# The last pair of token blocks of a fused recurrence and maxout layer as seven products, with stores by column halves

## The chip, the cores and the metric

The kernel runs on one core of one Trainium2 chip. The time is the device time of one execution in microseconds (us); medians of a few executions are quoted. Ratios are the mean time of one kernel's runs over that of the other's of the same rounds on the same chip, so they are not quite the ratio of the quoted medians. The span of a profile is about 1.8 us shorter than the timed value of the same execution. "Landing" means the moment at which a store's semaphore has had its last update, as the trace records it.

Engines in the profile: PE is TensorE (PEld its weight loads), DVE is VectorE, ACT is ScalarE, POOL is GpSimd, SP is SyncE, which here only issues DMAs and closes the program.

## The reference, cut to what matters

```python
# x, f_logit: (4, 6144, 256), lower_bound: (256,)
f = lower_bound + (1 - lower_bound) * sigmoid(f_logit)
h = 0
for t in range(S):                      # a gated recurrence over time
    h = f[:, t] * h + (1 - f[:, t]) * x[:, t]
    y[:, t] = h
# then, per token, with w1, w2: (256, 1024), w_out: (1024, 256)
g = maximum(y @ w1, y @ w2)
out = g @ w_out                         # (24576, 256) float32
```

The kernel writes the maximum as `y @ w1 + relu(y @ (w2 - w1))`. So the second layer has ten slices of 128 in its contraction: eight of ReLU outputs and two of `y` itself, whose weights `w13` are `w1 @ w_out`.

## The kernel before: the parts that matter here

Tokens go in blocks of 512. The second layer of two blocks, `ja` and `jb`, is one 2x2 by 2x2 block product: rows are the two blocks, the contraction is cut into two halves of five slices each, and the output columns into `lo` (0 to 127) and `hi` (128 to 255). That takes seven products of 20 matmuls of 128x128 in place of eight (the Strassen-Winograd scheme). A product adds into one bank of PSUM, the memory that matmuls write their sums to; the banks are named here X, B and E. VectorE makes four sums of left operands per pair, and `t1` to `t4` are sums of weights made once.

```python
def sevenths(p):
    ...
    product("X", part(0, 0), plain(0, lo), True)      # M1
    then(seed("B", "X"))                              # ACT: B = X
    product("E", sub(1), given(t1), True)             # M5
    then(snapshot("E", 5))                            # ACT: copy to SBUF
    product("X", sub(2), given(t2))                   # M6
    then(snapshot("X", 2))
    product("B", part(0, 1), plain(1, lo))            # M2: ja, lo is ready
    then(leave("B", ja, lo, None, False))
    product("X", sub(3), given(t3))                   # M7: jb, hi = X + snapshot 5
    then(leave("X", jb, hi, 5, False))
    product("E", sub(4), plain(1, hi))                # M3: ja, hi = E + snapshot 2
    then(leave("E", ja, hi, 2, True))
    product("X", part(1, 1), given(t4))               # M4: jb, lo
    then(leave("X", jb, lo, None, True))
```

The products of pair p are interleaved with the first layer of pair p + 1. The last pair has no successor and was done plainly instead, 40 matmuls of 128x256 per block; the last block was stored in four pieces of 128 KB, each as soon as its group of 128 tokens was copied:

```python
for step in queue: step()              # the rest of the pair before the last
for j in (NBLK - 2, NBLK - 1):
    for slot in range(FC):
        second_layer(j, slot)
# in second_layer, last block only, after the ten matmuls of token group i:
(nc.vector.tensor_copy if r else nc.scalar.copy)(out=osb[:, i:i+1, :], in_=ps[:, r:r+1, :])
store(j, osb, i, 1, nc.sync if r else nc.scalar)
```

## Time and profile before

The median was 380.87 us (three runs, 380.62 to 381.02). The page of the profile has the busy shares and the shares of the chain of waits that ended last:

```profile
span 379.8 us, 9454 instructions
...
PE 369.1 (97%) x4076; PEld 279.9 (74%) x4076; DVE 333.0 (88%) x402; ACT 300.3 (79%) x406; POOL 37.5 (10%) x79
...
PE 89%; DMA 4%; DVE 3%; POOL 1%; SPq 1%; ACT 0%; issue 0%
```

TensorE is busy 97% of the span and is 89% of the chain, so matmul work taken away should show, if it lies on the chain's end too. The chain from 360 us on (start, us, what):

```profile
365.36 1.51 PE ps L605 x27
366.87 8.75 PE ps L482 x80
375.62 0.02 issue
375.64 0.42 DVE osb L491
```

L605 is the matmul of the seven products, L482 the plain second layer. 27 narrow matmuls took 1.51 us, 56 ns each; the 80 wide ones took 8.75 us, 109 ns each. After the last VectorE copy (376.06) nothing is left but the last store and the closing, until 379.8. The timeline has the last ReLU and the last two copies (start, us, engine, line, what, and in brackets the idle time before it and who ended it):

```profile
365.40 1.02 ACT L444 ACTIVATE r<-dT 128x1024 f16<-128x1024 f32 x1 [0.79 <-PE dT L436]
...
374.55 0.37 ACT L491 COPY osb<-ps 128x256 f32<-128x256 f32 x1 [1.81 <-PE ps L482]
...
375.64 0.42 DVE L491 COPY osb<-ps 128x256 f32<-128x256 f32 x1 [1.76 <-PE ps L482]
```

These groups of the page give the durations of what the change adds: a sum, a snapshot and an add (after the shapes, the count, the busy us and the ns of one):

```profile
L506 DVE TENSOR_TENSOR S<-r 128x2560 f16<-128x2560 f16 x42 | 62.4, 1485 | 10.1 <-ACT r L444 10.0
...
L562 DVE TENSOR_TENSOR osb<-ps,sn 128x512 f32<-128x512 f32 x42 | 28.7, 684 | 6.8 <-ACT osb L560 5.3
...
L550 ACT COPY sn<-ps 128x512 f32<-128x512 f32 x42 | 24.6, 587 | 1.1 <-PE ps L605 0.9
```

Last, the end of the kernel in windows of half a microsecond; of each line the last three numbers matter, the granted clock, the mean busy share of the 16 DMA engines, and GB/s:

```profile
375.40:375.90 0.50, 0.20 (x2) 0.00 (x0) 0.26 (x1) 0.00 (x0) 0.00 (x0) 1.00 0.15 55
375.90:376.40 0.50, 0.00 (x0) 0.00 (x0) 0.16 (x1) 0.00 (x0) 0.00 (x0) 1.00 0.59 207
376.40:376.90 0.50, 0.00 (x0) 0.00 (x0) 0.00 (x0) 0.00 (x0) 0.00 (x0) 1.00 0.00 0
376.90:377.40 0.50, 0.00 (x0) 0.00 (x0) 0.00 (x0) 0.00 (x0) 0.00 (x0) 1.00 0.74 262
```

The DMA engines stand still from 376.4 to 376.9. The last store, issued at 376.09, then has them for itself.

### The profile page before, as it was taken

The numbers are of one execution on the slowest core, as the hardware profiler recorded it, in microseconds if no ns is written. First come the engines' busy times: TensorE is split into PE (matmuls) and PEld (weight loads), VectorE is DVE, ScalarE is ACT, GpSimd is POOL, SyncE is SP. The second block draws the span as 40 slices with busy tenths as digits, with TensorE's granted clock in tenths as the row PEclk, the third lists the DMA queues.
The fourth block names the chain that finished last, engine by engine and source line by source line (L and its number), as shares of the span: only waits on it lengthen the run. The fifth ranks groups of instructions, "written<-read, shape, count | busy, mean of one in ns | idle before, by whom it ended". The sixth has DMA issues, their size and how long they took to land.

```text
span 379.8 us, 9454 instructions
## 1 busy us (share of the span) xinstructions
PE 369.1 (97%) x4076; PEld 279.9 (74%) x4076; DVE 333.0 (88%) x402; ACT 300.3 (79%) x406; POOL 37.5 (10%) x79
## 2 busy tenths in 40 slices
PE   4999999999999999999999999999999999999995
PEld 3677766777777777777777777777777777777784
DVE  4696789999999999999999999999999999999721
ACT  4846788798798888888888887987888888888740
POOL 1500103101201101102011011011011021000000
PEclk9999999999999999999999999999999999999999
DMA  7994999989999999999899999999999999970223
GB/s 249 242 226 98 265 162 256 167 156 289 195 195 276 180 190 251 202 172 285 143 257 190 219 251 278 127 263 223 182 263 212 188 268 211 192 265 3 110 113 113
DMA packets 103389, 77.17 MB, mean 203 GB/s; under 512 B 93554, under 2 KB 94066, under 8 KB 102642
## 3 DMA queue, kind: packets, MB, share of 16 engines
q1 hardware_dynamic: 100514, 51.13, 59.8%
q0 software_dynamic: 2544, 25.17, 34.5%
q8 instruction: 32, 0.52, 0.6%
q10 hardware_dynamic: 288, 0.26, 0.2%
q14 instruction: 11, 0.09, 0.1%
HBM read 53.48 MB, written 48.23 MB: 268 GB/s over the span
## 4 chain that ended last, share of the span: by engine, by line
PE 89%; DMA 4%; DVE 3%; POOL 1%; SPq 1%; ACT 0%; issue 0%
PE ps L605 42%; PE dT L436 41%; PE ps L482 6%; DMA xT<-in_x_dram 3%; DMA r<-in_moe_w_dram 1%; DVE r L230 1%; DVE S L506 1%; SPq L117 0%; PE ps L180 0%; DVE osb L496 0%; DVE v L223 0%; POOL fT L105 0%; DVE ff L213 0%; ACT r L444 0%; POOL wob L631 0%
## 5 line engine op out<-in xcount | busy, mean ns | idle before, releaser
L444 ACT ACTIVATE r<-dT 128x1024 f16<-128x1024 f32 x192 | 195.8, 1022 | 53.2 <-PE dT L436 53.0
L436 PE MATMUL dT<-r,wd 128*128 128x512 f16 x768 | 225.4, 379 | 1.0 <-DVE wd L360 0.5
L605 PEld LDWEIGHTS <-S 128*128 128x128 f16 x1680 | 110.9, 101 | 37.6 <-issue 0.6
L605 PEld LDWEIGHTS <-r 128*128 128x128 f16 x1260 | 87.3, 101 | 36.6
L230 DVE TENSOR_TENSOR_SCAN r<-ff,r,v 128x512 f16<-128x512 f16 x88 | 108.2, 1270 | 0.8
L605 PE MATMUL ps<-t,S 128*128 128x128 f16 x1260 | 97.8, 219 | 0.0
L436 PEld LDWEIGHTS <-wd 128*128 128x128 f16 x768 | 67.6, 113 | 6.4 <-DVE wd L360 1.1
L506 DVE TENSOR_TENSOR S<-r 128x2560 f16<-128x2560 f16 x42 | 62.4, 1485 | 10.1 <-ACT r L444 10.0
L605 PE MATMUL ps<-wob,r 128*128 128x128 f16 x672 | 67.4, 219 | 0.0
L506 DVE TENSOR_TENSOR S<-r,S 128x2560 f16<-128x2560 f16 x42 | 61.9, 1474 | 0.0
L285 ACT ACTIVATE u<-fT 128x512 f16<-128x512 f16 x88 | 56.0, 636 | 1.0 <-DMA fT<-scr 1.0
L213 DVE TENSOR_SCALAR ff<-u,nom 128x512 f16<-128x512 f16 (+1 forms) x98 | 31.3, 346 | 9.7 <-ACT u L207 5.3
L348 POOL CAST waited<-fT 128x1 f32<-128x1 f16 x21 | 10.8, 513 | 279.5 <-DMA fT<-scr 279.5
L605 PE MATMUL ps<-w,r 128*128 128x128 f16 x168 | 36.8, 219 | 0.0
L562 DVE TENSOR_TENSOR osb<-ps,sn 128x512 f32<-128x512 f32 x42 | 28.7, 684 | 6.8 <-ACT osb L560 5.3
L605 PE MATMUL ps<-t,r 128*128 128x128 f16 x420 | 33.4, 219 | 0.0
L605 PE MATMUL ps<-wob,S 128*128 128x128 f16 x336 | 31.4, 219 | 0.0
L223 DVE TENSOR_TENSOR v<-u,xT 128x1024 f16<-128x1024 f16 x44 | 30.1, 684 | 0.2 <-DMA xT<-scr 0.2
L482 PEld LDWEIGHTS <-r 128*128 128x128 f16 x240 | 23.9, 101 | 6.9
L482 PE MATMUL ps<-wob,r 128*128 128x256 f16 x192 | 26.8, 273 | 0.0
L550 ACT COPY sn<-ps 128x512 f32<-128x512 f32 x42 | 24.6, 587 | 1.1 <-PE ps L605 0.9
L560 ACT COPY osb<-ps 128x512 f32<-128x512 f32 x42 | 24.4, 582 | 0.5 <-PE ps L605 0.5
(56 smaller groups left out, 134.8 us busy)
## 6 DMA issues: line engine op xcount, KB each, us to landing
out_dram<-osb SPq DMA_DIRECT2D x47, 512.0 KB, 3.9
scr<-in_f_logit_dram POOLq DMA_DIRECT2D x22, 512.0 KB, 7.4
scr<-in_x_dram POOLq DMA_DIRECT2D x22, 512.0 KB, 10.4
r<-in_moe_w_dram SPq DMA_DIRECT2D x4, 512.0 KB, 6.8
fT<-in_f_logit_dram POOLq DMA_DIRECT2D x3, 256.0 KB, 9.2
xT<-in_x_dram POOLq DMA_DIRECT2D x3, 256.0 KB, 11.1
osb<-in_f_logit_dram SPq DMA_DIRECT2D x2, 256.0 KB, 4.5
osb<-in_x_dram SPq DMA_DIRECT2D x2, 256.0 KB, 4.1
```

The lines of the kernel that those rows point to most:

```text
L213: nc.vector.tensor_scalar(out=ff[:, h, cols], in0=u[:, h, cols], scalar1=nom[:, h : h + 1], scalar2=1.0, op0=ALU.mult, op1=ALU.add,)
L223: nc.vector.tensor_tensor(out=like(v[:, :, cols], xT), in0=like(u[:, :, cols], xT), in1=xT, op=ALU.mult,)
L230: nc.vector.tensor_tensor_scan(out=y_of(j, h), data0=ff[:, h, o : o + TB], data1=v[:, h, o : o + TB], initial=0.0 if t0 == 0 else y_of(j - ...
L285: nc.scalar.activation(out=mids[p + NBLK, "u"][:, h, cols], in_=held[c, 0][:, h, cols], func=AF.Sigmoid, scale=-1.0,)
L436: nc.tensor.matmul(dT[:, fc % 2, :], lhsT=wd[:, kc, unit_cols(fc)], rhs=y_of(j, kc), start=(kc == 0), stop=(kc == KC - 1),)
L444: nc.scalar.activation(out=rts[j, k][:, g - 1 : g + 1, :].rearrange("p q (i m) -> p q i m", m=P), in_=dT[:].rearrange("p q (m i) -> p q i ...
L482: nc.tensor.matmul(ps[:, r, :], lhsT=left, rhs=right, start=(s == 0 and (r == 0 or j == NBLK - 1)), stop=(s == n - 1 and (r == 1 or j == N ...
L506: nc.vector.tensor_tensor(out=t[:], in0=a, in1=b, op=op)
L550: nc.scalar.copy(out=t[:], in_=bank[b][:])
L560: nc.scalar.copy(out=dst, in_=bank[b][:])
L562: nc.vector.tensor_tensor(out=dst, in0=bank[b][:], in1=snap[name][:], op=ALU.add)
L605: nc.tensor.matmul(bank[b][:, i, :], lhsT=a[:, k, cols], rhs=w, start=fresh, stop=after is not None, skip_group_check=True,)
```

## The change

The last pair becomes seven products as well. Its order is M1 M5 M2 M6 M3 M7 M4, so that each sum is ready in time. M4 does not add into bank X but goes to banks of its own; X is copied to a snapshot after M7, and `jb, lo` is formed in three adds as M4's token groups finish. Outputs leave by column halves, in pieces of 512 B. The third sum of the last pair is made while the first layer still runs.

```diff
-    def store(j, osb, first=0, n=TB // P, queue=None):
+    def store(j, osb, groups=slice(0, TB // P), cols=slice(0, D), queue=None):
 ...
+        end = p == NPAIR - 1
 ...
-                if last:
+                if end:
+                    store(j, osbs[j], cols=cols)
+                elif last:
                     store(j, osbs[j])
+        def leave_both(b):
+            def go():
+                leave(b, jb, hi, 5, False)()
+                snapshot(b, 4)()
+        def leave_last(i):
+            at = slice(0, 2) if i == 1 else slice(i, i + 1)
+            def go():
+                nc.vector.tensor_tensor(out=osbs[jb][:, at, lo],
+                    in0=bank["Y"][:, at, 0:P], in1=snap[4][:, at, :], op=ALU.add)
+                store(jb, osbs[jb], at, lo, nc.scalar if i == 2 else nc.sync)
 ...
+        if end:
+            product("B", part(0, 1), plain(1, lo))     # M2
+            then(leave("B", ja, lo, None, False))
+            product("X", sub(2), given(t2))            # M6
+            then(snapshot("X", 2))
+            product("E", sub(4), plain(1, hi))         # M3
+            then(leave("E", ja, hi, 2, True))
+            product("X", sub(3), given(t3))            # M7
+            then(leave_both("X"))
+            product("Y", part(1, 1), given(t4))        # M4, groups 0 and 1, 2, 3 in three banks
+            ... leave_last(1), (2), (3) after groups 1, 2, 3
 ...
-        for j in (NBLK - 2, NBLK - 1):
-            for slot in range(FC):
-                second_layer(j, slot)
+        sum1(p); sum2(p); sum4(p)
+        for step in sevenths(p):
+            step()
```

More of the change, by code (lines that the diff above doesn't have):

```diff
@@ L456, in store @@
             out=out[r0 : r0 + nb, :].rearrange("(p n) d -> p n d", p=P)[
-                :, first : first + n, :
+                :, groups, cols
             ],
-            in_=osb[:, first : first + n, :],
+            in_=osb[:, groups, cols],
         )
@@ L470, in second_layer @@
             g, r = divmod(i, 2)
-            if s == 0 and (r == 0 or j == NBLK - 1):
+            if s == 0 and r == 0:
                 acc["ps"] = ps_o.tile([P, 2, D], FP32, name="ps")
@@ L485, in second_layer @@
                 rhs=right,
-                start=(s == 0 and (r == 0 or j == NBLK - 1)),
-                stop=(s == n - 1 and (r == 1 or j == NBLK - 1)),
+                start=(s == 0 and r == 0),
+                stop=(s == n - 1 and r == 1),
                 skip_group_check=True,
             )
-            if j == NBLK - 1 and s == n - 1:
-                (nc.vector.tensor_copy if r else nc.scalar.copy)(
-                    out=osb[:, i : i + 1, :], in_=ps[:, r : r + 1, :]
-                )
-                store(j, osb, i, 1, nc.sync if r else nc.scalar)
-            elif r == 1 and s == n - 1:
+            if r == 1 and s == n - 1:
                 (nc.scalar.copy if j == 0 else nc.vector.tensor_copy)(
@@ L536, in then, with open_bank @@
             steps[-1][-1] = fn
-        def open_bank(b):
-            bank[b] = ps_o.tile([P, TB // P, P], FP32, name="ps")
+        def open_bank(b, i=0):
+            if i:
+                t = ps_d.tile([P, 2 * TB // P, P], FP32, name="dT")
+            else:
+                t = ps_o.tile([P, TB // P, P], FP32, name="ps")
+            bank[b] = t
         def seed(b, src):
@@ L564, in go @@
                     )
-                if last:
+                if end:
+                    store(j, osbs[j], cols=cols)
+                elif last:
                     store(j, osbs[j])
+            return go
+        def leave_both(b):
+            def go():
+                leave(b, jb, hi, 5, False)()
+                snapshot(b, 4)()
+            return go
+        def leave_last(i):
+            at = slice(0, 2) if i == 1 else slice(i, i + 1)
+            def go():
+                nc.vector.tensor_tensor(
+                    out=osbs[jb][:, at, lo],
+                    in0=bank["Y"][:, at, 0:P],
+                    in1=snap[4][:, at, :],
+                    op=ALU.add,
+                )
+                store(jb, osbs[jb], at, lo, nc.scalar if i == 2 else nc.sync)
             return go
@@ L585, in sevenths @@
         then(snapshot("E", 5))
-        product("X", sub(2), given(t2))
-        then(snapshot("X", 2))
-        product("B", part(0, 1), plain(1, lo))
-        then(leave("B", ja, lo, None, False))
-        product("X", sub(3), given(t3))
-        then(leave("X", jb, hi, 5, False))
-        product("E", sub(4), plain(1, hi))
-        then(leave("E", ja, hi, 2, True))
-        product("X", part(1, 1), given(t4))
-        then(leave("X", jb, lo, None, True))
+        if end:
[8 more added lines that the diff above has]
+            product("Y", part(1, 1), given(t4))
+            for i in range(TB // P):
+                steps[(i - TB // P) * (KH + 1)][-2] = i != 1
+                if i:
+                    steps[(i - TB // P + 1) * (KH + 1) - 1][-1] = leave_last(i)
+        else:
+            product("X", sub(2), given(t2))
+            then(snapshot("X", 2))
+            product("B", part(0, 1), plain(1, lo))
+            then(leave("B", ja, lo, None, False))
+            product("X", sub(3), given(t3))
+            then(leave("X", jb, hi, 5, False))
+            product("E", sub(4), plain(1, hi))
+            then(leave("E", ja, hi, 2, True))
+            product("X", part(1, 1), given(t4))
+            then(leave("X", jb, lo, None, True))
         def runner(step):
@@ L601, in run @@
                 if fresh:
-                    open_bank(b)
+                    open_bank(b, i)
                 a = left()
@@ L715 @@
             more = p + 1 < NPAIR
-            seq = [(27, scans[p]["scan10"]), (36, scans[p]["scan11"])]
+            seq = [
+                (27, scans[p]["scan10"]),
+                (36, scans[p]["scan11"]),
+                (112, lambda: sum3(p)),
+            ]
             if more:
@@ L723 @@
                     (84, scans[p + 1]["scan01"]),
-                    (112, lambda: sum3(p)),
                     (131, scans[p + 1]["decay1"]),
@@ L753 @@
             step()
-        for j in (NBLK - 2, NBLK - 1):
-            for slot in range(FC):
-                second_layer(j, slot)
+        p = NPAIR - 1
+        sum1(p)
+        sum2(p)
+        sum4(p)
+        for step in sevenths(p):
+            step()
 _INS = ['x', 'f_logit', 'lower_bound', 'moe_w1', 'moe_w2', 'moe_w_out']
```

## The prediction

> **What bounds the kernel now.** TensorE. On the page it is busy 97% of the span, and the chain of waits that ended last is 89% TensorE; in the windows from 300 us on it is busy without a gap. Only the end changes. The chain of 360-381 us reads: seven-product matmuls until 366.87, then 80 second-layer matmuls of 128x256 (8.75 us, 109 ns each) for the last two blocks, then a 424 ns VectorE copy until 376.06, then nothing but the last store and the closing: store issued 376.09, its 1 KB packets 376.93-377.44, landed 377.99, span end 379.77. So 3.7 us of tail follow the last copy.
>
> **What the change removes.** The 80 wide matmuls. Added are 140 of 128x128; in the same trace a run of 27 of these takes 1.51 us, 56 ns each, so 140 take 7.8 us. Matmul work saved: 0.95 us.
>
> **What it adds.**
> 1. Four sums on VectorE (1.48 us each). The third is moved into the last pair, where VectorE idles 5.3 us (timeline 358.6-363.9): free. The first needs the last ReLU, which ends 366.42. It runs about 366.45-367.94, while the first product (20 matmuls, 1.1 us from 366.65) is done at about 367.77: TensorE waits about 0.2 us before M5. The second (to 369.35) and fourth (to 370.75) are ready before M6 (370.3) and M7 (371.4). M2 before M6 is there for that.
> 2. A serial end. M3 ends about 373.75. VectorE adds out of its bank (0.69 us), and only then may ScalarE copy the same bank to the snapshot (0.59 us): the built program shows the copy waiting for VectorE. That is the rule of the Trainium skill, "PSUM — Partial Sum Buffer", section "PSUM bank collisions raise a hardware error": two engines may not read one bank at once. No run here shows a collision. So the snapshot is there at about 375.1. M4, in banks of its own, ends at 374.85 without waiting, and the adds of its groups queue behind the snapshot: 128x256 (estimate 0.42), then two of 128x128 (estimate 0.28 each, overlapping by 0.09 as VectorE neighbours do here): last one done about 375.95. TensorE ends 0.75 us earlier, but the last VectorE instruction only 0.1 us earlier.
> 3. Stores by column halves with 512 B pieces: 1 KB packets take 45 ns, 4 KB 160, so about 26 ns for 512 B (estimate); 256 KB is 0.8 us over 16 engines, not limiting. The last store is 64 KB in place of 128 KB, about 0.25 us less between first packet and landing, and its semaphore is checked one place later in the closing's list (0.07 us).
>
> **Sum.** 0.95 saved by matmuls, minus 0.2 (M5 wait), minus 0.6 (snapshot chain), plus 0.3 (smaller last store, closing): about 0.45 us, or 0.1%. All before 362 us is the same instruction stream.
>
> **Prediction: 380.4 us**, 8 in 10 between 379.9 and 380.9. Chances: faster by over 2% 0.005, within 2% 0.99, slower by over 2% 0.005.
>
> **What would show each step right.** No 128x256 matmuls after 367 us; 140 at a 56 ns pace; one TensorE gap of about 0.2 us before M5, released by the first sum, no other over 0.1 us; in the timeline VectorE add, ScalarE snapshot, VectorE adds back to back at the end, the chain of waits running through them; last VectorE end 0.1 us before that of the old kernel; last landing about 0.3 us earlier.
>
> **What would make it wrong.** The sum arriving later (a slower ReLU or leave ahead of it); 512 B pieces that cost more, or stores queued behind each other (each issue took 0.33 us), so that the last one lands later; semaphore hops above the 0.03 us seen between ReLU and sum[...].

(Two names are swapped in it: what it calls M7 and M3 are M3 and M7 in the names of the change. The instructions and times it means are the fifth and the sixth product.)

## The result

The changed kernel took 381.01 us (median of 4 runs, 380.54 to 381.83), before 380.87 (4 runs, 380.62 to 381.02): ratio 1.0007, 95% interval 0.9988 to 1.0025. That is 0.11 us outside the range predicted, with runs of one kernel that lie 1.3 us apart. A second set of six runs had a median of 380.66 us, inside that range, but before then had 380.69, ratio 1.0002 (0.9986 to 1.0017). So the part to explain is not the 0.1 us of the median: it is that the gain of 0.45 us is not there. The timed runs alone cannot exclude it (a gain of 0.45 us would be a ratio of 0.9988, the edge of both intervals); the traces have to show it.

The profiled spans, 379.8 us before and 379.1 after, seem to say that it is. They mislead. Matching ScalarE's activations of both traces one by one, the changed kernel is 0.66 us ahead at 27 us, long before any instruction that was changed, and still exactly 0.66 us ahead at the last ReLU: 365.40 and 364.74 us. Over the twelve other traces that lead over the trace of before lies between 0.21 and 0.97 us and is there by 27 us each time. The opening, which waits for the first loads, makes it: 0.47 us of it is the same in all twelve and arises between 22 and 26 us, where in the trace of before alone TensorE waits for a load of x. That execution took 381.55 us, more than any of the four timed runs of before. From here on every time is therefore counted from the start of the last ReLU of its own trace. From there to the end of the span it is 14.37 us before and 14.33 after.

The chain of the changed kernel at its end:

```profile
367.34 5.77 PE ps L642 x100
373.12 0.02 issue
373.14 0.70 DVE osb L562
373.84 0.02 issue
373.87 0.60 ACT sn L550
374.46 0.02 issue
374.48 0.42 DVE osb L582
```

And its timeline, with the last ReLU, the one gap of TensorE, and the end:

```profile
364.74 1.02 ACT L444 ACTIVATE r<-dT 128x1024 f16<-128x1024 f32 x1 [0.79 <-PE dT L436]
...
367.34 1.14 PEld L642 LDWEIGHTS <-S 128*128 128x128 f16 x20 [0.17 <-DVE S L501]
...
373.14 0.69 DVE L562 TENSOR_TENSOR osb<-ps,sn 128x512 f32<-128x512 f32 x1 [0.37 <-PE ps L642]
373.50 0.72 PE L642 MATMUL dT<-t,r 128*128 128x128 f16 x10
373.87 0.59 ACT L550 COPY sn<-ps 128x512 f32<-128x512 f32 x1 [2.37 <-DVE osb L562]
374.48 0.42 DVE L582 TENSOR_TENSOR osb<-ps,sn 128x256 f32<-128x256 f32 x1 [0.65 <-ACT sn L550]
374.83 0.48 DVE L582 TENSOR_TENSOR osb<-dT,sn 128x128 f32<-128x128 f32 x2
375.14 0.37 ACTq L455 DMA_DIRECT2D out_dram<-osb  x1
```

This much is as predicted: one TensorE gap of 0.17 us before M5 released by the first sum, then no gap; M4 done at 374.22; VectorE add, ScalarE snapshot and VectorE adds back to back. The windows of the DMA engines are not:

```profile
374.74:375.24 0.50, 0.00 (x0) 0.00 (x0) 0.50 (x3) 0.00 (x0) 0.00 (x0) 1.00 0.71 203
375.24:375.74 0.50, 0.00 (x0) 0.00 (x0) 0.07 (x1) 0.00 (x0) 0.00 (x0) 1.00 0.95 282
375.74:376.24 0.50, 0.00 (x0) 0.00 (x0) 0.00 (x0) 0.00 (x0) 0.00 (x0) 1.00 0.97 293
376.24:376.74 0.50, 0.00 (x0) 0.00 (x0) 0.00 (x0) 0.00 (x0) 0.00 (x0) 1.00 0.89 281
376.74:377.24 0.50, 0.00 (x0) 0.00 (x0) 0.00 (x0) 0.00 (x0) 0.00 (x0) 1.00 0.33 98
```

Where before they stood still ahead of the last store, they are now at work without a break from about 375.1 to 377.0, at 281 to 293 GB/s.

The account, in us after the start of the last ReLU. The two measured columns come from the traces' records; the predicted one is worked out from the prediction's times minus 365.40 (its landing: 12.60, less 0.10 for the adds and 0.25 for the store):

| | before | predicted | after |
|---|---|---|---|
| TensorE done | 10.21 | 9.45 | 9.48 |
| last copy or add done | 10.67 | 10.55 | 10.57 |
| last store issued | 10.69 | | 10.69 |
| last packet done | 12.03 | | 12.28 |
| last landing | 12.60 | 12.25 | 12.67 |
| end of the span | 14.37 | 13.9 | 14.33 |

TensorE is done 0.73 us earlier, of which 0.10 us reaches the last add: right. From the last add to the landing it takes 2.10 us, where 1.93 less 0.25, or 1.68, was predicted: 0.42 us more. The closing, 1.78 us before, is 1.66 us. So the 0.04 us that the stage gains are 0.10 (adds) less 0.17 (stores) plus 0.12 (closing).

### The profile page after: what moved, and what is told of

The parts are those of the page before. It is cut to its first block, busy times and chain, and to the rows that moved or that the text cites. A ratio compares the mean times of both kernels' runs of the same rounds, so it can differ in the third digit from the quotient of the medians.

```text
span 379.1 us, 9589 instructions
## 1 busy us (share of the span) xinstructions
PE 367.8 (97%) x4136; PEld 279.5 (74%) x4136; DVE 338.9 (89%) x407; ACT 302.6 (80%) x409; POOL 34.9 (9%) x79
## 4 chain that ended last, share of the span: by engine, by line
PE 91%; DVE 5%; DMA 1%; ACT 1%; SPq 0%; issue 0%; DVEq 0%
PE ps L642 44%; PE dT L436 41%; PE ps L482 4%; DVE r L230 1%; DMA osb<-in_f_logit_dram 1%; DVE S L501 1%; PE ps L180 1%; DVE wd L360 1%; DVE v L223 0%; PE ps L392 0%; DVE ff L213 0%; DVE osb L491 0%; ACT r L444 0%; DVE r L264 0%; SPq L117 0%
## 5 line engine op out<-in xcount | busy, mean ns | idle before, releaser
L642 PEld LDWEIGHTS <-S 128*128 128x128 f16 x1760 | 115.4, 101 | 37.9 <-issue 0.6
L642 PEld LDWEIGHTS <-r 128*128 128x128 f16 x1320 | 90.8, 101 | 36.6
L642 PE MATMUL ps<-t,S 128*128 128x128 f16 x1320 | 101.6, 219 | 0.0
L501 DVE TENSOR_TENSOR S<-r 128x2560 f16<-128x2560 f16 x44 | 65.4, 1486 | 14.5 <-ACT r L444 14.4
L642 PE MATMUL ps<-wob,r 128*128 128x128 f16 x704 | 69.8, 219 | 0.0
L501 DVE TENSOR_TENSOR S<-r,S 128x2560 f16<-128x2560 f16 x44 | 65.1, 1479 | 0.0
L642 PE MATMUL ps<-w,r 128*128 128x128 f16 x176 | 38.5, 219 | 0.0
L348 POOL CAST waited<-fT 128x1 f32<-128x1 f16 x21 | 8.7, 413 | 280.0 <-DMA fT<-scr 280.0
L550 ACT COPY sn<-ps 128x512 f32<-128x512 f32 x45 | 26.4, 587 | 4.6 <-DVE osb L562 2.4
L482 PEld LDWEIGHTS <-r 128*128 128x128 f16 x160 | 16.0, 101 | 6.2
L642 PE MATMUL ps<-w,S 128*128 128x128 f16 x88 | 19.3, 219 | 0.0
## 6 DMA issues: line engine op xcount, KB each, us to landing
xT<-in_x_dram POOLq DMA_DIRECT2D x3, 256.0 KB, 10.3
```

The costliest lines, as they stand in the source:

```text
L482: nc.tensor.matmul(ps[:, r, :], lhsT=left, rhs=right, start=(s == 0 and r == 0), stop=(s == n - 1 and r == 1), skip_group_check=True,)
L501: nc.vector.tensor_tensor(out=t[:], in0=a, in1=b, op=op)
L550: nc.scalar.copy(out=t[:], in_=bank[b][:])
L642: nc.tensor.matmul(bank[b][:, i, :], lhsT=a[:, k, cols], rhs=w, start=fresh, stop=after is not None, skip_group_check=True,)
```

## The experiments

Three theories for what sets the end:

- A: the last stores share the DMA engines, and the last one leaves behind the others. A1 blames the small pieces, A2 that many bytes become ready late.
- B: the chain of add, snapshot and adds sets it, and the stores follow at a fixed distance.
- C: separate from both, the closing costs more or less, depending on which semaphore the last store signals. It came up with the fourth run.

All results, in one table. "Add", "packet", "landing" and "end" are the last ones, in us after the last ReLU's start, from one profile each. "Pieces" are the stretches of memory that a store is cut into; each is one packet in the trace. Ratios are to before in the same rounds.

| run | median us (n) | before (n) | ratio, 95% | add | packet | landing | end |
|---|---|---|---|---|---|---|---|
| before | 380.87 (4) | | | 10.67 | 12.03 | 12.60 | 14.37 |
| after | 381.01 (4) | 380.87 (4) | 1.0007, 0.9988-1.0025 | 10.57 | 12.28 | 12.67 | 14.33 |
| e1_again | 380.66 (6) | 380.69 (11) | 1.0002, 0.9986-1.0017 | 10.57 | 12.27 | 12.67 | 14.30 |
| e2_nohi | 380.67 (5) | 380.69 (11) | 0.9996, 0.9984-1.0008 | 10.57 | 12.16 | 12.55 | 14.28 |
| e3_order | 381.07 (6) | 380.69 (11) | 1.0012, 0.9996-1.0027 | 10.13 | 12.56 | 12.95 | 14.61 |
| e4_rows | 380.64 (6) | 380.69 (11) | 1.0000, 0.9985-1.0014 | 10.57 | 12.61 | 13.18 | 14.11 |
| e5_slot_before | 380.36 (5) | 380.73 (11) | 0.9989, 0.9976-1.0001 | 10.67 | 12.04 | 12.71 | 13.64 |
| e6_slot_after | 380.61 (6) | 380.73 (11) | 1.0000, 0.9987-1.0013 | 10.57 | 12.62 | 13.25 | 14.16 |
| e7_lastonly | 379.93 (4) | 380.73 (11) | 0.9975, 0.9962-0.9988 | 10.56 | 11.86 | 12.24 | 13.41 |
| e8_split | 379.83 (5) | 380.73 (11) | 0.9978, 0.9966-0.9990 | 9.96 | 12.00 | 12.58 | 13.51 |
| e9_slot_after_act | 380.00 (5) | 380.70 (9) | 0.9980, 0.9967-0.9992 | 10.57 | 12.27 | 12.72 | 13.63 |
| e10_order_q | 381.28 (4) | 380.70 (9) | 1.0019, 1.0003-1.0034 | 10.14 | 12.72 | 13.15 | 14.84 |
| e11_split_hi | 379.87 (5) | 380.70 (9) | 0.9975, 0.9963-0.9988 | 9.96 | 12.22 | 12.75 | 13.66 |

The outputs were right except in e2 and e7, which leave out stores on purpose.

### e1: the changed kernel again

> The changed kernel once more, for more rounds and a second profile. Both theories: from the start of the last ReLU to the end of the span 14.3 us again (before 14.37), whatever the opening does; between rounds the whole span may move by half a microsecond, since the two profiles on hand differ by 0.66 us that is there at 27 us and stays the same to 365 us. Ratio to before within 0.998 to 1.002.

The stage repeats to 0.03 us (14.33 and 14.30), add, packet and landing to 0.01, while the start of the last ReLU moved by 0.21 us. So differences of a tenth in the last add and the last packet can be read from single profiles, which the timed medians could not settle. The closing and the landing proved looser: the kernel before landed at 12.60, and in e5, which changes nothing near its end but semaphores, at 12.71.

### e2: without the store of the right half of block b

```diff
-                    store(j, osbs[j], cols=cols)
+                    if j == ja or cols == lo:
+                        store(j, osbs[j], cols=cols)
```

> The changed kernel without the 256 KB store of the last block's right half, wrong on purpose. Theory A (the last stores queue behind one another in the DMA engines, 1,024 pieces of 512 B from 10.3 us to 12.3 us after the last ReLU's start): the last landing comes 0.4 us earlier, at about 12.3 us, and the end at 13.9 us. Theory B (the chain VectorE add, ScalarE snapshot, VectorE adds sets the end, the stores follow at a fixed distance): nothing changes, end at 14.3 us.

The landing came 0.12 us earlier (the last packet 0.11), not 0.4 (theory A) and not 0 (theory B). Without this store the DMA engines were idle from 10.3 to 11.0 us, then busy until 12.16 all the same. So the store of 256 KB ahead is the smaller part. The three stores after the adds fill that last stretch by themselves: 128, 64 and 64 KB, 512 packets of about 26 ns, 0.83 us for 16 engines as an estimate and 1.05 us from the first to the last in the trace (11.11 to 12.16). All three are issued within 0.5 us, because the first waits for the snapshot.

### e3: M7 before M3

```diff
+            product("X", sub(2), given(t2))     # M6
+            then(snapshot("X", 2))
             product("B", part(0, 1), plain(1, lo))
             then(leave("B", ja, lo, None, False))
-            product("X", sub(2), given(t2))
-            then(snapshot("X", 2))
+            product("X", sub(3), given(t3))     # M7
+            then(leave_both("X"))
             product("E", sub(4), plain(1, hi))  # M3
             then(leave("E", ja, hi, 2, True))
-            product("X", sub(3), given(t3))
-            then(leave_both("X"))
```

> M7 before M3, as in the other pairs: M1 M5 M6 M2 M7 M3 M4. The snapshot for the last adds is then taken while M3 runs, so the serial chain is gone; M6 waits about 0.3 us for the second sum. The last VectorE add should end 0.45 us earlier (10.1 us after the last ReLU's start, in place of 10.57). Theory B: the end follows, 13.9 us. Theory A: the 256 KB that leave after the sixth product and the 256 KB of M4 still fall into the last 2 us, so the end is 14.2 to 14.4 us all the same.

Its chain at the end, to be set against that of the changed kernel above:

```profile
369.20 4.65 PE ps L642 x80
373.85 0.02 issue
373.88 0.58 DVE osb L562
374.46 0.04 issue
374.50 0.62 DVE osb L582 x2
```

The snapshot is gone from the chain, and with its last ReLU at 365.19 the last add is done at 10.13, 0.43 us earlier than in the changed kernel. The end is 0.29 us later. Theory B has fallen: an earlier last add did not bring an earlier end. A's number (14.2 to 14.4) was passed as well. Two things differ besides the chain. The last add was done at 10.13 but its store was issued at 10.71, because SyncE was still issuing the stores before it. And TensorE, which now waits for the second sum before M6, is done 0.29 us later (9.77), so the last 512 KB become ready later. In the packet records the last 1,024 pieces of 512 B take 1.96 us from the first to the last in both kernels: from 10.31 to 12.28 in the changed one, from 10.60 to 12.56 here. The later start is the whole difference.

### e10: the same with one store on another queue

```diff
-                    store(j, osbs[j], cols=cols)
+                    store(j, osbs[j], cols=cols, queue=nc.scalar if cols == hi and j == ja else nc.sync)
```

> e3 (M7 before M3, no serial chain) with the store of block a's right half moved from SyncE's to ScalarE's queue. In e3 the last add ended at 10.13 us but its store was issued at 10.71, since SyncE was busy issuing stores of 256 and 512 pieces (0.53 to 0.59 us each). Issue theory: last issue at 10.2 to 10.3 us, last landing 12.45 us (e3: 12.95). DMA-work theory (from 10.6 us on 1,024 pieces of 512 B have to pass, 1.66 us for 16 engines): last packet not before 12.25, last landing 12.65 us.

The last store was indeed issued 0.45 us earlier (10.26), and it landed 0.19 us later. So the issue time on SyncE was not what held e3 back. Nor did two queues save issue time in sum: the four last issues took 0.70, 0.40, 0.63 and 0.62 us, together 2.34, against 0.53, 0.59, 0.42 and 0.55, together 2.09, for the same four stores in e3. The Trainium skill, "DMA: Bandwidth & Descriptors", section "Issuing engines are not separate DMA queues", says that several issuing engines only save the sequencer's time to start a DMA. This case agrees in that the end did not come earlier; the issues overlapped, but three of the four took longer. The last packet (12.72) was later than the sum of the DMA work expected (12.25). The packet records show why: the last 1,024 pieces take 1.96 us here too, 267 GB/s, not 1.66, since 26 ns is the time of one packet and leaves out the gaps between packets; and the first of them left at 10.76, 0.16 us later than in e3.

### e4: stores by whole rows

```diff
-                if end:
-                    store(j, osbs[j], cols=cols)
-                elif last:
+                if last:
                     store(j, osbs[j])
 ...
-                store(jb, osbs[jb], at, lo, nc.scalar if i == 2 else nc.sync)
+                store(jb, osbs[jb], at, queue=nc.scalar if i == 2 else nc.sync)
```

> The changed kernel with its stores by whole rows: block a in one store of 512 KB after M3, block b in three stores of 2 KB and 1 KB pieces after the groups' adds, none after M7. Theory A1 (the small pieces cost the time): the last packet leaves at about 11.9 us after the last ReLU's start in place of 12.28, end 14.0 to 14.1 us. Theory A2 (bytes that become ready late cost it; 512 KB start only at about 11.0 us): last packet at 12.4, end at 14.5 us. Theory B: end at 14.2 to 14.3 us, as the adds end where they did.

The last packet is far from A1's 11.9 and past A2's 12.4: 512 KB that start only at 11.0 us end at 12.6, longer pieces or not. The end is where A1 put it, but by accident, as the landing shows: the end came 0.2 us earlier than in the changed kernel although the landing was 0.5 us later. From landing to end it took 0.93 us, against 1.66. SyncE's records in the trace show why. At the end it waits for eight DMA semaphores one after the other, in fixed order. Stores take the eight in turn. If the last store signals the first of them, the seven other checks come after the landing; if it signals the last, they are done before it.

### e5 and e6: other semaphores for the last store, by tiny loads

Seven (e5, in the kernel before) or six (e6, in the changed one) loads of 8 bytes, put into the middle of the program, move the turn on (e6's edit is shown):

```diff
+                if slot == 8 and p in (14, 15, 16, 17, 18, 19):
+                    nc.sync.dma_start(out=tiny[0:1, 2*(p-14) : 2*(p-14)+2], in_=lower_bound[0:2])
```

> The kernel before, with seven tiny loads (8 B each) put into the middle of the program, so that the last store signals the last of the eight semaphores that the closing waits for, one after another, instead of the first. Theory C (the closing costs about 1.75 us after the last landing when the landing is first in that list, and 0.93 us when it is last, as in e4): last landing 12.6 us after the last ReLU's start as before, end at 13.5 us in place of 14.37, time 0.8 us less. Rival: e4's short closing came from something else in that kernel: end at 14.3 us.

> The changed kernel with six such tiny loads, so that its last store too signals the last semaphore of the list. Theory C: last landing 12.67 us as in the changed kernel, end at 13.6 us. With the same place in the list as e5 the two kernels then differ by the landing alone, 0.05 to 0.1 us in favour of the old one: the change gains nothing even so.

e5 did about what was expected (12.6 and 13.5): landing 12.71, end 13.64, which is 0.73 us less than before, by moving nothing but a turn, and with it a pause of SyncE that e6 brought to light. In the timed runs it is 0.11% (interval 0.9976 to 1.0001), not clear of noise by itself.

e6 missed. Its last store was issued at 11.04 in place of 10.69 and landed at 13.25. SyncE had paused, with nothing to wait for: from the end of one instruction to the start of the next it took 0.36 us, and the next was the wait ahead of that store. In eleven of the thirteen traces such a pause of 0.34 to 0.37 us stands in front of the same place in SyncE's stream, its 208th recorded instruction; in the other two (e4, e8) a wait for a landing covers that place. In e6 the six loads with their waits had moved the last store to that place.

### e9: the tiny loads on ScalarE's queue

```diff
-                    nc.sync.dma_start(out=tiny...
+                    nc.scalar.dma_start(out=tiny...
```

> e6 again with the six tiny loads issued by ScalarE's queue, so that SyncE's own instructions keep their number. In all ten traces so far SyncE pauses about 0.35 us before its 208th recorded instruction, whichever that is; in e6 it was the one that starts the last store, which is why that landed at 13.25. Theory C with this pause: the pause is back in the closing's list ahead of the last semaphore, where it is hidden; last landing 12.65 to 12.7 us as in the changed kernel, end at 13.6 us. Rival (the tiny loads or the place of the semaphore make the last store late): last landing at 13.2 us again. Time against before: 0.7 us less.

So it was (though of the ten traces that the text counts, e4 and e8 don't show the pause): landing 12.72, end 13.63, time 0.20% less than before (interval 0.9967 to 0.9992). The pause is now in the closing ahead of the landing and costs nothing. These are SyncE's eight closing waits from the traces' records (us after the last ReLU's start; the time is when the wait was passed, the asterisk marks the semaphore of the last store):

```
before  12.61*  12.68  12.74  12.83  12.91  12.98  13.05  13.42    end 14.37
after   12.51   12.69* 12.76  13.13  13.22  13.29  13.35  13.42    end 14.33
e5      11.47   11.55  11.62  11.69  11.75  11.81  11.87  12.73*   end 13.64
e9      11.25   11.32  11.39  11.76  11.85  12.28  12.49  12.74*   end 13.63
```

The step of 0.37 us in the first two rows (13.05 to 13.42, 12.76 to 13.13) is the pause. The last two rows also give the cleanest comparison of the change: with the same place in the list, the kernel before and the changed one end at 13.64 and 13.63 and land at 12.71 and 12.72. In the traces the change is worth nothing. The timed ratios of e5 and e9 (0.9989 and 0.9980) are from different rounds and chips, and their intervals overlap; they do not settle it.

### e7: only the two last stores of block b

```diff
-                    store(j, osbs[j], cols=cols)
+                    if j == ja:
+                        store(j, osbs[j], cols=cols)
 ...
-                store(jb, osbs[jb], at, lo, nc.scalar if i == 2 else nc.sync)
+                if i > 1:
+                    store(jb, osbs[jb], at, lo, nc.scalar if i == 2 else nc.sync)
```

> The changed kernel without the store of block b's right half and without the store of groups 0 and 1, wrong on purpose: only the two last stores of 64 KB are left after the adds. Its last store happens to signal the last semaphore of the list. Theory A (the last stores share the DMA engines: 512 packets of 26 ns come within 0.5 us, 0.83 us of work for 16 engines, and the last store leaves behind them): last packet at 11.7 us after the last ReLU's start in place of 12.28, last landing at 12.1 to 12.2 us in place of 12.67, so 0.45 us as the prediction had counted for a last store of half the size. Rival (issue and first-byte time of small-piece stores alone set it): last packet not before 12.0 us.

The last packet (11.86) lies between the two theories' numbers (11.7, and not before 12.0), but the gap in the work of the DMA engines ahead of the last stores is back, as these windows show (last ReLU at 364.91):

```profile
374.91:375.41 0.50, 0.00 (x0) 0.00 (x0) 0.50 (x3) 0.00 (x0) 0.00 (x0) 1.00 0.35 107
375.41:375.91 0.50, 0.00 (x0) 0.00 (x0) 0.06 (x1) 0.00 (x0) 0.00 (x0) 1.00 0.00 0
375.91:376.41 0.50, 0.00 (x0) 0.00 (x0) 0.00 (x0) 0.00 (x0) 0.00 (x0) 1.00 0.37 116
376.41:376.91 0.50, 0.00 (x0) 0.00 (x0) 0.00 (x0) 0.00 (x0) 0.00 (x0) 1.00 0.48 147
```

The last landing is at 12.24 us, 0.42 us earlier than in the changed kernel, and close to the landing the prediction had counted with (12.25). 0.12 us of this is what e2 had gained already. The other 0.31 us come with the store of groups 0 and 1, by its packets in front (about 0.2 us) and because SyncE issued the last store 0.10 us earlier. This shows the cause: the other stores of the same half microsecond stand in front of the last one. From its issue to its first packet the last store takes 1.19 us in the changed kernel, 1.08 in e2 and 0.87 in e7 (0.83 before); from the first packet to the landing it takes 0.79, 0.79 and 0.78. The end (13.41) is not comparable with that of the changed kernel, since the place in the closing differs.

### e8: bank X in two halves

The accumulator X of the last pair lies in two banks, token groups 0 and 1 in one, 2 and 3 in the other. Snapshot and right half of the first two groups leave while M7 still runs on the other two. ScalarE copies each half first, then VectorE adds; stores go by whole rows as in e4.

```diff
+        def half(b, i):
+            return b + "23" if end and b == "X" and i > 1 else b
+        def leave_half(b, at):
+            def go():
+                snap_half(4, b, at)               # ACT: copy half of X
+                nc.vector.tensor_tensor(out=osbs[jb][:, at, hi], in0=bank[b][:, at, :],
+                                        in1=snap[5][:, at, :], op=ALU.add)
 ...
             product("X", sub(3), given(t3))
-            then(leave_both("X"))
+            steps[-2 * (KH + 1) - 1][-1] = leave_half("X", slice(0, 2))
+            then(leave_half("X23", slice(2, 4)))
```

> A version that may beat both: the accumulator of M1, M6, M7 of the last pair lies in two banks by token groups, so that the snapshot and the right half of groups 0 and 1 leave while TensorE works on groups 2 and 3; stores by whole rows as in e4; last semaphore of the list as in e4. Theory A: the three stores of block b start about 0.6 us earlier than in e4 (first add after M4 at 8.95 to 9.2 us, not 9.75), last packet at 11.8 to 12.0 us, last landing at 12.2 to 12.5 us, end at 13.1 to 13.4 us, about 1.1 us less than before. Theory B as a rival for what sets the end (the last add plus a fixed distance of 3.76 us, as in the changed kernel): last add at 9.9 us and end at 13.7 us.

The last add is 0.61 us earlier than in the changed kernel and the last packet at 12.00, as expected; the landing (12.58) and with it the end (13.51) were 0.1 us later than expected. In the timed runs e8 has 379.83 us against 380.73, 0.22% less (interval 0.9966 to 0.9990). It is faster than the kernel before (the changed kernel was not run in these rounds; its stage ends at 14.33), but mind where that comes from: its landing, 12.58 us, is where it was before the change (12.60), and the 0.86 us of its end are the closing. That the last add came 0.71 us earlier than before was again lost to the DMA engines.

### e11: e8 with the right half stored early

```diff
                 in1=snap[5][:, at, :], op=ALU.add)
+                store(jb, osbs[jb], at, hi)
 ...
-                store(jb, osbs[jb], at, queue=nc.scalar if i == 2 else nc.sync)
+                store(jb, osbs[jb], at, lo, nc.scalar if i == 2 else nc.sync)
```

(and six tiny loads on ScalarE's queue, so that the last store signals the last semaphore of the list.)

> e8 with the right half of block b stored as soon as it is added, in two stores of 256 pieces of 512 B, and six tiny loads on ScalarE's queue so that the last store signals the last semaphore again. DMA-work theory: 256 KB leave before the adds of M4 are there, so fewer bytes stand in front of the last store; but 512 B pieces take 26 ns against 45 ns for 1 KB, so all the work from 8.9 us on (512 KB in 4 KB pieces, 1.28 us, and 1,024 small pieces, 1.66 us) ends at 11.85 to 12.0 us: last landing 12.25 to 12.5 us, end at 13.2 to 13.4 us, at best 0.3 us before e8 (13.51). If only the order of the bytes counted: last packet 11.5 us.

The adds are where they were in e8, and the right half is issued from 8.70 us on in place of 9.59, yet the last packet is 0.22 us later, and packet, landing and end all miss the expectation by 0.2 to 0.3 us. Here too the last 1,024 pieces took 1.98 us and not the 1.66 that it had counted with. The windows of e8, from 10.5 us after the last ReLU on:

```profile
374.97:375.47 0.50, 0.00 (x0) 0.00 (x0) 0.00 (x0) 0.00 (x0) 0.00 (x0) 1.00 1.02 385
375.47:375.97 0.50, 0.00 (x0) 0.00 (x0) 0.00 (x0) 0.00 (x0) 0.00 (x0) 1.00 0.93 342
375.97:376.47 0.50, 0.00 (x0) 0.00 (x0) 0.00 (x0) 0.00 (x0) 0.00 (x0) 1.00 0.78 281
```

and the same windows of e11:

```profile
374.97:375.47 0.50, 0.00 (x0) 0.00 (x0) 0.00 (x0) 0.00 (x0) 0.00 (x0) 1.00 1.02 283
375.47:375.97 0.50, 0.00 (x0) 0.00 (x0) 0.00 (x0) 0.00 (x0) 0.00 (x0) 1.00 1.02 280
375.97:376.47 0.50, 0.00 (x0) 0.00 (x0) 0.00 (x0) 0.00 (x0) 0.00 (x0) 1.00 1.03 286
```

The engines are busy up to the last packet in both (e8's leaves at 376.47), but pieces of 512 B pass at about 283 GB/s, those of 2 KB and 1 KB at up to 385. So A1 has its part too: storing earlier is paid for with the smaller pieces that it needs. In the timed runs the two cancel (0.9978 and 0.9975, each against before in its own rounds).

## Why the prediction was wrong

**What was right.** TensorE bound everything up to its last matmul; 140 narrow matmuls in place of 80 wide ones ended it 0.73 us earlier (0.75 predicted). The wait before M5 was 0.17 us (0.2). The serial end was found in the built program before any run: VectorE add, then ScalarE snapshot of the same bank, then the adds, last one 0.10 us earlier than before (0.1 predicted). The order follows the rule in the Trainium skill, "PSUM — Partial Sum Buffer", section "PSUM bank collisions raise a hardware error"; the trace agrees that the copy starts only after the add (373.83, 373.87), and no run shows a collision.

**The step that failed.** "256 KB is 0.8 us over 16 engines, not limiting." With this the prediction costed the last store as if it were alone. But the snapshot, which the same text had found, holds back the add of groups 0 and 1 until 10.17 us, so the last three stores, 256 KB together, are issued within half a microsecond, behind another 256 KB. The next clause, "The last store is 64 KB in place of 128 KB, about 0.25 us less between first packet and landing", was right taken by itself: that stretch went from 1.07 to 0.79 us. What it missed lies ahead of the first packet. From the last add to the issue it takes 0.12 us in place of 0.03, because SyncE is still issuing the store before; from the issue to the first packet 1.19 in place of 0.83, because that store's packets go first (its last one ends at 11.84, the last store's first one starts at 11.87). So the time from the last add to the landing changed by plus 0.17 us (1.93 to 2.10) in place of minus 0.25. e7 takes the other stores of block b away, and both terms go back to 0.03 and 0.87 us; that its landing meets the predicted one to 0.01 us is in part luck, since single landings vary by 0.1. e2 shows that the earlier 256 KB are 0.12 us of it. The prediction had named "stores queued behind each other" among the things that would make it wrong, but had given them no cost.

**The remedy that did not follow.** It would have been wrong to conclude that the snapshot chain costs the gain. e3 removes it and gains the 0.43 us at the last add, but TensorE ends 0.29 us later there, the last 512 KB start that much later, and the end follows them. e8 gains 0.61 us at the last add without that, and its landing is still only 0.09 us earlier than in the changed kernel.

**The closing.** The prediction gave the change of place in the closing's list 0.07 us. That one place is worth about that (0.06 to 0.09 us), but the closing went from 1.78 to 1.66 us. The lever behind it was missed: six or seven places, and a pause of SyncE, are worth 0.73 us (e5), more than the change's whole expected gain.

**The range.** Half a microsecond to either side was too narrow for a comparison of two medians of four runs: the opening alone moved the start of the last ReLU by up to 0.97 us between the traces. A range for a gain of 0.45 us has to hold this as well.

**Left open.** Why the time from last packet to last landing differs (0.39 us in the changed kernel, 0.56 before, 0.67 in e5, 0.63 in e6), what SyncE's pause is, and what sets the pace of the 512 B pieces: 1,024 of them took 1.96 to 1.98 us in six traces (the changed kernel, e1, e3, e9, e10 and e11), although the mean of the packets' own times, 26 to 29 ns, differs between those traces. So it is not shown whether the engines themselves or what feeds them is the limit.

## What to carry to other kernels

At the end of a kernel, cost the stores together: add up the bytes of all stores that are issued within the last two microseconds at the measured GB/s for pieces of their size, and ask when the engines are through with them, before crediting a shorter matmul or a smaller last store. When one stage is compared, count from an event close to it in each trace, since the opening can differ between runs by more than the effect. And look at the closing list once: which semaphore the last store signals was worth 0.7 us here, more than the change itself, for a few tiny loads; but check the trace, since in e6 the same loads delayed the last store.

## What the Trainium skill lacked or had wrong

- "DMA: Bandwidth & Descriptors", section "Specifications": the page gives 512 B as the smallest size for line rate. Stores from SBUF to HBM in 512 B pieces kept the 16 engines busy at 280 to 286 GB/s, with 28 ns per packet, those in 4 KB pieces at 401 GB/s with 161 ns (both in e11).
- "DMA: Bandwidth & Descriptors", section "Issuing engines are not separate DMA queues": the section has no durations of issues by the number of pieces. Here the four last stores took 2.34 us of issue time in sum on two queues (e10) against 2.09 us mostly on one (e3). And a store of 128 long pieces took 0.33 us to issue, one of 512 pieces 0.53 to 0.65 us. From the start of the issue to the first packet, with the engines idle, it took 0.83 us for 128 pieces (before, e4) and 1.19 to 1.29 us for 512 (the changed kernel).
- No page has the closing's list of DMA semaphores: from the last landing to the end of the span 1.6 to 1.8 us when the last store signals the first or second of eight, 0.91 to 0.93 us when it signals the last (e4, e5, e6, e8, e9, e11; 1.16 us in e7, where SyncE's pause fell there).
- "Runtime: NRT & Kernel Launch", section "Instruction fetch mechanics", calls the cost of passing from one block of instructions to the next mostly hidden. In every trace here where no wait covers it, SyncE pauses for 0.34 to 0.37 us before its 208th recorded instruction, and in e6 that delayed the last store. Whether it is that block boundary was not tested; what the traces add is that in all thirteen an 8 KB packet of an instruction queue starts 0.5 to 1.1 us after that place.
